# Two DMA transposes of u moved ahead of score transposes on the sync queue, at the start of a fused attention and feed-forward kernel

## The chip, the cores and the metric

One core of one Trainium2 chip. The metric is device time in microseconds (us). Each timing below gives a median and a range over several executions. A kernel and the kernel before it, when compared, ran on the same chip in the same rounds.

"PE" is TensorE's matrix multiply, "PEld" its weight loads, "DVE" is VectorE, "ACT" is ScalarE, "POOL" is GpSimd, and "SP" is SyncE, which here does nothing but issue DMA transposes (and four first loads). Every execution lists the mean granted TensorE clock over its span; 1.000 means that its clock record holds no slowed piece in the span to speak of. (A record can begin late: that of the trace of before begins at 10.4 us and says nothing of the time until then.)

## The reference

Eight batches of attention with squared-ReLU scores, gated by u, then a feed-forward layer with x cos(x):

```python
scores = (1/S) * z @ z.T              # B=8, S=3008, d_qk=64
attn   = maximum(scores, 0) ** 2
x      = u * (attn @ v)               # D=256
h      = x @ w_in                     # 256 -> 2048
out    = (h * cos(h)) @ w_out         # 2048 -> 256
```

The score matrix is symmetric, and the kernel uses that: away from the first batch's first columns it computes only half of the score blocks and gets the rest by DMA transposes.

## The kernel before

The sequence of 3008 rows is cut in six columns of 512 (the last has 448). For each column `c` of batch 0 the scores of blocks (c, R) are computed by PE, passed through ReLU by ACT (or DVE), and squared by DVE into a score buffer `a`. For c = 0, 1, 2 all six blocks are computed directly. Blocks with R = 3, 4, 5 are also transposed, because columns 3 to 5 will use the transposed copy `tt`.

```python
apool = pool("a", 9)        # score buffers
tpool = pool("at", 13)      # transposed score buffers
utpool = pool("ut", 3)      # transposed u
ps_acc = psum("ps_acc", NDH)  # two accumulators, one column at a time
...
def s_squares(b, c, R, p, banks):
    if p == 0:
        halves[(b, c, R)] = apool.tile([P, K, K, P], FP16, name="a")
    t = halves[(b, c, R)]
    ...                                                  # ReLU: rt <- banks
    nc.vector.tensor_tensor(
        t.rearrange("p s k w -> p k s w")[:, 2 * p:2 * p + 2], rv, rv, ALU.mult)
    if p == 1:
        ...
        if R > c and not direct(b, R, c):
            tt = tpool.tile([P, K, K, P], FP16, name="tt")
            turned[(b, c, R)] = tt
            nc.sync.dma_start_transpose(tt..., t...)     # a score transpose
```

A column ends with a multiply by u on DVE, which reads both accumulators out. It needs u with rows and columns exchanged, and that is a DMA transpose on the same sync queue:

```python
def turn_u(b, c):
    ut = utpool.tile([P, NDH, CW], FP16, name="ut")
    hold(nc.sync.dma_start_transpose(ut..., ust[c % 2]...))
    uts[(b, c)] = ut

def finish():      # after the last acc matmul of the column
    ...
    nc.vector.tensor_tensor(x[:, nh, :], acc[nh][:, o:o + n], ut[:, nh, o:o + n], ALU.mult)
```

The program is a list of events, each with a time in abstract units (8 units to a column), emitted in order of that time:

```python
for c in range(NC):
    at(t + c * U + (1 if b or c not in (1, 2) else -3 * c), 0, lambda b=b, c=c: turn_u(b, c))
for q in range(4):
    at(4 + 2 * q, 0, lambda q=q: load_w_in(q))           # loads by POOL
    at(17 + 2.5 * q, 0, lambda q=q: load_w_out(q))
```

In what follows u0, u1, u2 are the transposes of u for columns 0, 1, 2. s1, s2, ... are the score transposes in their order of issue: s1 to s3 are of column 0 (R = 3, 4, 5), s4 to s6 of column 1. With nine score buffers, a square takes the buffer of the square nine places before it. So the square of block (2, 4) needs the buffer that s3 reads from, and the one two places after column 2's last block that of s6. A square cannot start before that transpose has landed.

Of the kernel before, what the change touches and what calls it, by code (L numbers as in the profile page):

```python
# [14 lines left out]
def kernel(  # L15
# [31 lines left out]
    U = 8  # L47
# [37 lines left out]
    def hold(dma):  # L85

        after(dma.ins, gate[0] if gate else before[-1], SYNC)
# [13 lines left out]
    def load_z(b):  # L101
        for g in range(NG):
            n, full, rest = rows(z, b, g)
            j0 = g * G + 1
            load(zst[:, j0:j0 + n, :], full)
            if rest is not None:
                for p0 in (0, JLAST):
                    load(zst[p0:p0 + JLAST, j0 + n, :], rest)

    def turn_z(b):  # L110
        for k in range(2):
            n = (NJ + 2) // 2 - k
            hold(nc.sync.dma_start_transpose(
                zT[b % 2][:, k:k + 2 * n - 1:2, :],
                zst[:, k:k + 2 * n, :].rearrange("p j d -> p (j d)")))

    def load_v(b, g):
        t = vs(b, g)
        n, full, rest = rows(v, b, g)
        load(t[:, 0:n, :], full)  # L120
        if rest is not None:
            for p0 in (0, JLAST):
                load(t[p0:p0 + JLAST, n, :], rest)

    def load_w_in(q):
        fs = slice(q * CW, (q + 1) * CW)
        load(w_in16[:, :, fs], moe_w_in[:, fs].rearrange("(k p) f -> p k f", p=P))

    def load_w_out(q):
        n = NFT // 4  # L130
        load(w_out16[:, q * n:(q + 1) * n, :],
             moe_w_out[q * n * P:(q + 1) * n * P, :].rearrange("(k p) f -> p k f", p=P))
# [3 lines left out]
    def load_u(b, c):  # L136
        r0 = c * CW
        n = min(K, (S - r0) // P)
        st = ust[c % 2]
        for dh in range(NDH):  # L140
            ds = slice(dh * P, (dh + 1) * P)
            load(
                st[:, dh, 0:n, :],
                u[b, r0:r0 + n * P, ds].rearrange("(j p) d -> p j d", p=P))
            if n < K:
                load(st[0:JLAST, dh, n, :], u[b, r0 + n * P:S, ds])

    def turn_u(b, c):
        ut = utpool.tile([P, NDH, CW], FP16, name="ut")
        hold(nc.sync.dma_start_transpose(  # L150
            ut.rearrange("p h (j w) -> p (h j) w", w=P),
            ust[c % 2].rearrange("p h j w -> p (h j w)")))
        uts[(b, c)] = ut
# [17 lines left out]
    def first_z_load(g):  # L171
        zfs[g] = xpool.tile([P, NDH, TW], FP16, name="x")
        zf = zfs[g].rearrange("p h w -> p (h w)").bitcast(FP32).rearrange(
            "p (j d) -> p j d", d=dqk)
        zfs[g] = zf
        n, full, rest = rows(z, 0, g)
        nc.sync.dma_start(zf[:, 0:n // 2, :], full[:, 0:n // 2, :])
        nc.scalar.dma_start(zf[:, n // 2:n, :], full[:, n // 2:n, :])
        if rest is not None:
            nc.scalar.dma_start(zf[0:JLAST, n, :], rest)  # L180
            nc.sync.dma_start(zf[JLAST:P, n, :], rest)

    def first_z_turn(g):
        j0 = g * G
        last = g == NG - 1
        nc.vector.tensor_copy(zst[:, j0 + 1:j0 + 1 + G, :], zfs[g])  # L186
        for k, n in ((0, G), (G, 1))[0:1 + last]:
            tp = ps_w.tile([P, CW], FP32, name="w").bitcast(FP16).rearrange(
                "p (j w) -> p j w", w=P)
            for i in range(n):  # L190
                chain(nc.tensor.transpose(  # L191
                    tp[:, i, :],
                    zst[:, j0 + k + i:j0 + k + i + 2, :].rearrange("p j d -> p (j d)"),
                    ident))
            if g < 2:
                nc.scalar.copy(zT[0][:, j0 + k:j0 + k + n, :], tp[:, 0:n, :])  # L196
            else:
                nc.vector.tensor_copy(zT[0][:, j0 + k:j0 + k + n, :], tp[:, 0:n, :])
# [181 lines left out]
    def at(t, rank, f):  # L380
        events.append((t, rank, len(events), f))
# [11 lines left out]
    for b in range(B):  # L393
        pairs = [(b, c, R, p) for c, R in groups for p in range(2)]
        for i in range(0, len(pairs), NV):
            some = [pr for pr in pairs[i:i + NV] if not direct(*pr[:3])]
            t = b * span - lead + span * i / len(pairs)
# [11 lines left out]
    for b in range(B):  # L409
        for c in range(NC):  # L410
            t = b * span + c * U
# [16 lines left out]
    for m in range(NT):  # L428
        b, i = divmod((m + 1) * TW - 1, S)
# [7 lines left out]
    for b in range(B):  # L437
        t = b * span
        if b == 0:
            for g in range(NG):  # L440
                at(-100 + g, 0, lambda g=g: first_z_load(g))
                at((-30, -2.5, 0.8)[g], 0, lambda g=g: first_z_turn(g))
            first = [lambda: load_v(0, 0), lambda: load_u(0, 0), lambda: load_v(0, 1),
                     lambda: load_v(0, 2), lambda: load_u(0, 1)]
            for i, f in enumerate(first):
                at(-80 + i, 0, f)
            at(-70, 0, gate.clear)
            at(2, 0, lambda: load_u(0, 2))
            for q in range(4):
                at(4 + 2 * q, 0, lambda q=q: load_w_in(q))  # L450
                at(17 + 2.5 * q, 0, lambda q=q: load_w_out(q))
        else:
            at(t - 3.5 * U, 0, lambda b=b: load_z(b))
            at(t - 2.5 * U, 0, lambda b=b: turn_z(b))
            for g in range(NG):
                at(t + (-1.5, -0.4, -0.1)[g] * U, 0, lambda b=b, g=g: load_v(b, g))
        for c in range(3 if b == 0 else 0, NC):
            at(t + (c - 1.25) * U, 0, lambda b=b, c=c: load_u(b, c))
        for c in range(NC):
            at(t + c * U + (1 if b or c not in (1, 2) else -3 * c), 0, lambda b=b, c=c: turn_u(b, c))  # L460
    dummy = kpool.tile([P, 1], FP32, name="dummy")

    def prepare():
# [49 lines left out]
```

## Time and profile before

| kernel before | |
|---|---|
| three runs | 1247.27 us median, 1246.61 to 1248.53 |
| profiled span | 1244.6 us |
| PE busy | 1234.4 us, 99% of the span |
| PE gaps of over 0.15 us between 12 and 75 us | 2.63 us, then 1.33 us in four pieces |
| PE gaps of over 0.15 us after that | none |

The page of the profile of before. The first line is busy time by engine. The other is the chain of work that ended last, as shares of the span (here and below, "issue" is time in which the engine waited for nothing that the profile shows, and DVEq and ACTq are the sequencers of these engines):

```profile
PE 1234.4 (99%) x7533; PEld 680.0 (55%) x7533; DVE 782.0 (63%) x1389; ACT 844.7 (68%) x1609; POOL 145.8 (12%) x201
...
PE 97%; DMA 2%; DVE 0%; ACT 0%; issue 0%; DVEq 0%; ACTq 0%
```

So only PE's few gaps are to be had. The timeline of PE, before. Columns: start, duration, engine, line, operation, out<-in, shapes, count, and in brackets the idle time before it and what ended it:

```profile
38.29 1.46 PE L310 MATMUL acc<-a,v_65 128*128 128x512 f16 x6
39.68 0.60 PE L223 MATMUL w<-zT_63 64*128 64x512 f16 x4
42.91 1.46 PE L310 MATMUL acc<-a,v_66 128*128 128x512 f16 x6 [2.63 <-DVE x L331]
...
61.42 0.45 PE L223 MATMUL w<-zT_63 64*128 64x512 f16 x2 [0.23 <-DVE g L351]
62.62 1.89 PE L344 MATMUL w<-x,w_in_70 128*128 128x512 f16 x8 [0.75 <-DVE g L351]
```

Column 1's last acc matmuls end at 39.75. Column 2 cannot start until the multiply (line 331) has emptied the accumulators. Call this the first gap, and the group at 54 to 63 us the second gap. The timeline of DVE, before, shows why:

```profile
38.42 1.29 DVE L258 TENSOR_TENSOR a<-rt 128x1024 f16<-128x1024 f16 x2 [0.17 <-ACT rt L256]
42.17 1.29 DVE L331 TENSOR_TENSOR x<-acc,ut 128x512 f16<-128x512 f32 x2 [2.46 <-DMA ut<-ust_62]
...
58.88 0.69 DVE L258 TENSOR_TENSOR a<-rt 128x1024 f16<-128x1024 f16 x1 [2.06 <-ACT c_739 L348]
```

The square of block (2, 3) runs at 38.42 without a wait for a transpose. The multiply waits 2.46 us for u1. The last line names ACT's c_739, which this square does not read: line 351 reads it, at 60.69. The ReLU that the square does read had ended by 57.08. c_739 happens to end at 58.80, just as s6 lands, and so the bracket has the wrong name. When a wait is on several semaphores, the chain of waits is the better witness. The chain of waits, before, in order of time (start, duration, what):

```profile
31.03 11.05 DMA ut<-ust_62
...
42.17 0.70 DVE x L331
42.87 0.04 issue
42.91 1.46 PE acc L310 x6
...
47.39 11.40 DMA tt<-a
58.79 0.03 issue
58.82 0.02 DVEq L258
58.84 0.04 issue
58.88 0.17 DVE a L258
```

u1 lands at 42.08 and s6 at 58.79, each just before the work that waited for it.

How DMA transposes and loads get on together shows in the sums by window, before. The columns after the window and its length are PE, PEld, DVE, ACT and POOL busy, granted clock, DMA share (over 1 when packets overlap), and GB/s:

```profile
28.00:38.00 10.00, 10.00 (x53) 3.46 (x52) 8.62 (x14) 7.00 (x14) 0.70 (x1) 1.00 1.35 133
42.00:44.00 2.00, 1.09 (x6) 0.48 (x5) 1.83 (x4) 0.00 (x0) 1.36 (x2) 1.00 1.21 260
```

From 28 to 38 us loads (of w_in, and the last of u2's) and transposes share the engines and move 133 GB/s together. From 42 to 44 us there are only transposes, at 260 GB/s. The Trainium skill, "DMA: Bandwidth & Descriptors", section "Latency and other measured facts", gives 261 GB/s for the DMA transposes of one kernel. These two us agree with it; the trace after moved more, 286 GB/s, from 44 to 46 us, also with transposes alone.

### The profile page before, as it was taken

Reading aid. Unit: us, or ns where it says so; the run is one execution under the profiler, and the core shown is the slowest. Engines: PE = TensorE matmul, PEld = TensorE weight load, DVE = VectorE, ACT = ScalarE, POOL = GpSimd, SP = SyncE. Lnnn points to the kernel's source line nnn. Section 1 sums busy time; section 2 is a strip of 40 time slices with the busy share of each in tenths; the row PEclk is TensorE's granted clock in tenths of the full one; section 3 lists DMA queues with packets and bytes.
Section 4 is the critical chain, followed back from the end, with each engine's and each line's share of the span. In section 5 each row is a group of like instructions: output and inputs, shape, how many; then the busy total and the mean of one; then the engine's idle time right before and its main releaser. Section 6 shows DMA issues by size and latency. Waiting matters only on the chain.

```text
span 1244.6 us, 20404 instructions
## 1 busy us (share of the span) xinstructions
PE 1234.4 (99%) x7533; PEld 680.0 (55%) x7533; DVE 782.0 (63%) x1389; ACT 844.7 (68%) x1609; POOL 145.8 (12%) x201
## 2 busy tenths in 40 slices
PE   9899999999999999999999999999999999999998
PEld 3355555555555555555555555555555555555556
DVE  7766666666666666656666566665666656666555
ACT  6666676666676766667766667766667766667646
POOL 3210101001010010100101011011010111100000
PEclk9999999999999999999999999999999999999999
DMA  9997958679576795757958569685695957957311
GB/s 162 152 174 129 141 91 119 114 122 142 99 117 111 117 144 106 115 111 110 149 101 121 107 109 150 101 129 99 109 158 92 129 101 112 152 101 108 72 33 45
DMA packets 484212, 144.85 MB, mean 116 GB/s; under 512 B 432400, under 2 KB 484112, under 8 KB 484112
## 3 DMA queue, kind: packets, MB, share of 16 engines
q1 hardware_dynamic: 356448, 88.73, 43.1%
q0 software_dynamic: 100400, 29.77, 24.7%
q10 hardware_dynamic: 27264, 25.06, 6.3%
q8 instruction: 59, 0.97, 0.3%
q14 instruction: 41, 0.34, 0.1%
HBM read 60.29 MB, written 24.64 MB: 68 GB/s over the span
## 4 chain that ended last, share of the span: by engine, by line
PE 97%; DMA 2%; DVE 0%; ACT 0%; issue 0%; DVEq 0%; ACTq 0%
PE acc L310 37%; PE w L361 26%; PE w L344 26%; PE w L223 6%; DMA tt<-a 1%; DMA ut<-ust_62 1%; PE acc L285 1%; DMA x<-in_z_dram 0%; DVE g L351 0%; PE w L191 0%; DVE x L331 0%; ACT zT_63 L196 0%; ACT rt L256 0%; DVE a L258 0%; DVE zst L186 0%
## 5 line engine op out<-in xcount | busy, mean ns | idle before, releaser
L361 PE MATMUL w<-w_out_71,g 128*128 128x256 f16 x3008 | 448.6, 273 | 0.0
L344 PE MATMUL w<-x,w_in_70 128*128 128x512 f16 x1504 | 445.6, 379 | 0.8 <-DVE g L351 0.8
L361 PEld LDWEIGHTS <-g 128*128 128x128 f16 x3008 | 294.2, 98 | 191.6 <-issue 1.4
L256 ACT ACTIVATE rt<-w 128x512 f16<-128x512 f32 x489 | 253.1, 613 | 121.2 <-PE w L223 121.2
L258 DVE TENSOR_TENSOR a<-rt 128x1024 f16<-128x1024 f16 x254 | 173.8, 691 | 180.8 <-ACT rt L256 178.3
L344 PEld LDWEIGHTS <-w_in_70 128*128 128x128 f16 x1504 | 147.0, 98 | 59.2 <-issue 3.9
L90 POOL DMA_DIRECT2D ust_62<-in_u_dram x64 | 44.7, 704 | 385.8 <-PE acc L310 355.9
L240 ACT ACTIVATE rt<-w 128x512 f16<-128x512 f32 (+3 forms) x176 | 62.8, 449 | 39.7 <-PE w L223 39.7
L331 DVE TENSOR_TENSOR x<-acc,ut 128x64 f16<-128x64 f32 (+7 forms) x178 | 69.6, 431 | 29.1 <-PE acc L310 26.6
L310 PE MATMUL acc<-a,v_65 128*128 128x512 f16 x336 | 85.8, 380 | 0.0
L310 PEld LDWEIGHTS <-v_66 128*128 128x128 f16 x552 | 51.9, 98 | 61.8 <-issue 14.1
L310 PEld LDWEIGHTS <-v_65 128*128 128x128 f16 x552 | 51.6, 98 | 60.0 <-issue 13.1
L310 PEld LDWEIGHTS <-v_67 128*128 128x128 f16 x552 | 51.9, 98 | 58.7 <-issue 11.1
L310 PEld LDWEIGHTS <-v_68 128*128 128x128 f16 x552 | 51.9, 98 | 57.7 <-issue 10.9
L310 PE MATMUL acc<-a,v_66 128*128 128x512 f16 x312 | 79.4, 379 | 2.6 <-DVE x L331 2.6
L310 PE MATMUL acc<-a,v_68 128*128 128x512 f16 x312 | 79.2, 379 | 0.0
L310 PE MATMUL acc<-a,v_67 128*128 128x512 f16 x312 | 79.1, 379 | 0.0
L368 ACT ACTIVATE ob<-w 128x256 f32<-128x256 f32 x188 | 73.0, 388 | 5.3 <-PE w L361 5.3
L241 DVE TENSOR_TENSOR a<-rt 128x512 f16<-128x512 f16 (+3 forms) x176 | 47.3, 321 | 44.0 <-ACT rt L240 44.0
L90 POOL DMA_DIRECT2D ust_61<-in_u_dram x48 | 36.5, 766 | 224.4 <-PE acc L310 206.7
L310 PE MATMUL acc<-tt,v_68 128*128 128x512 f16 (+1 forms) x240 | 62.2, 371 | 0.0
L310 PE MATMUL acc<-tt,v_67 128*128 128x512 f16 (+1 forms) x240 | 62.1, 371 | 0.0
(1546 smaller groups left out, 1399.8 us busy)
## 6 DMA issues: line engine op xcount, KB each, us to landing
out_dram<-ob ACTq DMA_DIRECT2D x92, 256.0 KB, 2.3
ust_61<-in_u_dram POOLq DMA_DIRECT2D x48, 128.0 KB, 4.0
ust_62<-in_u_dram POOLq DMA_DIRECT2D x32, 128.0 KB, 4.4
a<-a SPq DMA_TRANSPOSE x132, 3.0
v_65<-in_v_dram POOLq DMA_DIRECT2D x4, 512.0 KB, 6.1
v_66<-in_v_dram POOLq DMA_DIRECT2D x4, 512.0 KB, 6.6
v_68<-in_v_dram POOLq DMA_DIRECT2D x4, 512.0 KB, 6.2
v_67<-in_v_dram POOLq DMA_DIRECT2D x4, 512.0 KB, 6.2
```

What stands on the lines that cost most here:

```text
L90: hold(nc.gpsimd.dma_start(dst, src))
L223: chain(nc.tensor.matmul(sp[:, s0 * P:], zt[h, R * K + k + 1 - lo, :], zt[h, j0 + s0:j0 + K, :].rearrange("p j w -> p (j w)"), start=True, ...
L240: nc.scalar.activation(rt[:, i, k * P:], banks[k][:, k * P:], AF.Relu)
L241: nc.vector.tensor_tensor(t[:, k, k:, :].rearrange("p s w -> p (s w)"), rt[:, i, k * P:], rt[:, i, k * P:], ALU.mult)
L256: nc.scalar.activation(rt[:, i, :], banks[k], AF.Relu)
L258: nc.vector.tensor_tensor(t.rearrange("p s k w -> p k s w")[:, 2 * p:2 * p + 2], rv, rv, ALU.mult)
L285: chain(nc.tensor.matmul(accs[(b, c)][nh], vs(b, NG - 1)[h, G - 1, nh * P:(nh + 1) * P], a[h], start=False, stop=False))
L310: chain(nc.tensor.matmul(acc[nh][:, 0:wn], vs(b, j // G)[:, j % G, nh * P:(nh + 1) * P], a, start=(n == 0), stop=(n == NJ - 2)))
L331: nc.vector.tensor_tensor(x[:, nh, :], acc[nh][:, o:o + n], ut[:, nh, o:o + n], ALU.mult)
L344: chain(nc.tensor.matmul(hp, w_in16[:, k, ft * P:(ft + 1) * P], x[:, k, :], start=(k == 0), stop=(k == NDH - 1)))
L361: chain(nc.tensor.matmul(ys[m][:, 0:D], gs[(m, f4)][:, ft % FG, ts * P:(ts + 1) * P], w_out16[:, ft, :], start=(ft == 0), stop=(ft == NFT ...
L368: nc.scalar.activation(obs[m][:, i, :], ys[m][:, 0:D], AF.Copy, bias=0.0, scale=inv_s2)
```

## The change

u1's transpose had its source in place at 18.6 us but was issued at 31.0 us, behind three score transposes. The intent is to issue it, and u2, earlier, so that the multiply never waits.

```diff
-            at(t + c * U + (1 if b or c not in (1, 2) else -3 * c), 0, lambda b=b, c=c: turn_u(b, c))
+            at({(0, 1): 1.01, (0, 2): 6.5}.get((b, c), t + c * U + 1), 0, lambda b=b, c=c: turn_u(b, c))
```

The instruction order on all other engines stays the same. On the sync queue it goes from u0, s1, s2, s3, **u1**, s4, **u2**, s5, s6 to u0, **u1**, s1, s2, s3, **u2**, s4, s5, s6.

## The prediction

> **What bounds the kernel now.** TensorE. The page gives PE 1234.4 of a span of 1244.6 us (99%), at full granted clock; the chain of waits is 97% PE. So nothing can gain more than the few PE gaps. PE's timeline shows, after the start, two: 2.63 us at 40.2-42.9 us (first acc matmul of column 2, released by the gating multiply on DVE), and a cluster at 54-62.6 us (0.20 + 0.16 + 0.23 + 0.75 = 1.34 us, on DVE). After that PE is never idle for over 0.15 us at once.
>
> **First gap.** The multiply of column 1 sat 2.46 us on the transposed u of column 1. That transpose stands behind three score transposes in the sync queue; it is issued at 31.0-35.3 and lands at 42.08. Its source had landed at 18.6. This is what the change aims at.
>
> **Second gap.** In the chain, DVE's square at 58.88 waits for the sixth score transpose (issued 47.4, landed 58.79), which frees a score buffer (of 9). DVE was idle 2.06 us, then ran behind.
>
> **What the change does.** No work is added or removed; only the sync queue's order differs. Before: u0, s1, s2, s3, u1, s4, u2, s5, s6. After: u0, u1, s1, s2, s3, u2, s4, s5, s6. From 17.7 to 80 us this queue issues with hardly a pause (1.2 to 7.4 us each), DMA share mostly above 1: it is bound by throughput. The Trainium skill, "DMA: Bandwidth & Descriptors", section "Issuing engines are not separate DMA queues", says DMAs of all issuers share 16 engines and interleave; the trace agrees: the u2 transpose landed in 3.2 us where no loads ran (42.0), u1's in 11.0 beside the w_in loads.
>
> **Costing.** u1 must wait for its load (18.6), then lands near 22-24, needed at 39.7: -2.6 us. s1-s3 slip by one u transpose (1-4 us). s3 frees the buffer of a square that will be wanted at about 41.3 (43.97 less 2.63); it landed at 41.05, will land near 42: a DVE wait of about 1 us, mostly hidden from PE. Ahead of s6 stands the same set of transposes as before, so it still lands near 58-59.5, while its buffer is now wanted 2.6 us earlier (about 54.2). Also the fourth column's u load, which had waited for u1, and the PE-gated w_out and z loads come earlier and compete. So DVE's wait there grows from 2 to about 4 us, and the PE gaps after it from 1.3 to 2.5-4 us: most of the gain is given back.
>
> **Prediction.** Net -0.9 us: **1246.4 us**, 8 in 10 between **1244.3 and 1248.3** (the runs before spread 1.9 us). Faster by over 2%: 0.01; within 2%: 0.98; slower by over 2%: 0.01.
>
> **What would show it.** Right: u1's transpose lands before 27 us; the multiply no longer waits for it; PE's gap at 40 us is under 1 us; a DVE square waits over 3 us for a score transpose at 54-59 us, and PE's gaps between 44 and 65 us total 2 to 4 us. Wrong: if s6 lands 2 us or more earlier, the second wait does not grow and the full 2.6 us arrives (1244.6). If s3 lands after 43.5, a PE gap stays at 41-44 us.
>
> **What would make it wrong.** How loads and transposes share the DMA engines is judged from one trace; 1-2 us on s6 moves the total one for one. If s6 lands after 60, the kernel is about 1 us slower. A later stage fed by transposes (from 80 us) could start to stall, which I don't expect.

A note on one figure: "where no loads ran" holds from 42 to 44 us; the packets of the next loads began before u2 landed at 45.20.

## The result, and the profile after

1247.86 us median of four runs (1246.64 to 1250.69), against 1247.53 us of four runs of before. A ratio is worked out from the fast runs of the same rounds, so it is not quite the ratio of these medians. It is 1.001, with a 95% interval of 0.9995 to 1.0025: no gain. The forecast gain of 0.9 us did not come. The profiled execution was the fastest of the four.

The timeline of PE, after:

```profile
37.66 1.03 PE L310 MATMUL acc<-a,v 128*128 128x512 f16 x4
38.62 0.60 PE L223 MATMUL w<-zT 64*128 64x512 f16 x4
41.69 2.45 PE L310 MATMUL acc<-a,v 128*128 128x512 f16 x6 [2.46 <-DVE x L331]
44.07 1.04 PE L223 MATMUL w<-zT 64*128 64x512 f16 x4
...
61.71 0.37 PE L223 MATMUL w<-zT 64*128 64x512 f16 x1 [0.25 <-ACT rt L256]
```

The first gap is still there, 2.46 us, released by the same multiply. And the six matmuls after it took 2.45 us, against 1.46 us before. The timeline of DVE, after:

```profile
39.74 1.29 DVE L258 TENSOR_TENSOR a<-rt 128x1024 f16<-128x1024 f16 x2 [2.55 <-ACT rt L256]
40.95 1.28 DVE L331 TENSOR_TENSOR x<-acc,ut 128x512 f16<-128x512 f32 x2
42.15 0.68 DVE L254 TENSOR_SCALAR rt<-w 128x512 f16<-128x512 f32 x1
43.87 1.29 DVE L258 TENSOR_TENSOR a<-rt 128x1024 f16<-128x1024 f16 x2 [1.04 <-DMA tt<-a]
...
57.47 0.69 DVE L258 TENSOR_TENSOR a<-rt 128x1024 f16<-128x1024 f16 x1 [0.28 <-ACT rt L256]
```

The multiply no longer waits for anything of its own. The square ahead of it in DVE's order, block (2, 3), does: 2.55 us. Again the bracket names ACT, whose ReLUs for this block had ended by 37.81, and the chain of waits, after, names the real one:

```profile
23.98 15.67 DMA tt<-a
39.65 0.03 issue
39.67 0.02 DVEq L258
...
40.95 0.69 DVE x L331
41.65 0.04 issue
41.69 2.45 PE acc L310 x6
```

That DMA is s2. It was issued at 23.98 and landed at 39.65; before, the same transpose landed at 27.62. (The last line of DVE above is the square that needs the buffer of s6: it did not wait for it.) The issues of DMA in narrow windows show s2 in both. Columns: out<-in, queue, operation, count, us from issue to landing. Before, a window in which s2 alone is being issued on the sync queue:

```profile
tt<-a SPq DMA_TRANSPOSE x1, 6.5
```

and after:

```profile
tt<-a SPq DMA_TRANSPOSE x1, 15.7
```

The sums by window, after, columns as above, and below it the last of these windows in before:

```profile
28.00:38.00 10.00, 10.00 (x53) 3.51 (x52) 7.80 (x13) 6.86 (x14) 2.19 (x3) 1.00 1.41 118
42.00:46.00 4.00, 4.00 (x14) 1.00 (x12) 2.95 (x6) 1.29 (x3) 0.57 (x1) 0.57 1.38 250
```

```profile
42.00:46.00 4.00, 3.09 (x16) 1.10 (x15) 3.83 (x7) 1.28 (x3) 2.23 (x3) 1.00 0.94 169
```

The granted clock was 0.57 from 42 to 46 us, against 1.00 before. The clock record of the trace has one piece at half speed there, from 42.0 to 45.4 us. The landings of all these transposes, read from the traces (us):

| | u0 | u1 | s1 | s2 | s3 | s4 | u2 | s5 | s6 |
|---|---|---|---|---|---|---|---|---|---|
| before | 21.40 | 42.08 | 23.09 | 27.62 | 41.05 | 43.86 | 45.20 | 52.78 | 58.79 |
| after | 19.61 | 21.88 | 30.73 | 39.65 | 43.77 | 46.17 | 44.44 | 52.34 | 56.99 |

u1 came 20.2 us earlier. s2 came 12.0 us later and s1 7.6 us later. Two things add up for s1. Its issue had to wait behind u1, which had to wait for its own load (landed at 18.80), so it began at 20.53 instead of 17.66 us. And from then on the loads of u2 and w_in were in flight too. For s2 the packets show it. Before, s2 was issued at 21.13 us, and from 20 to 25 us the sync queue moved 0.91 MB and the loads next to nothing. From 25 to 28 us, in both traces, the loads took the DMA engines: a share of 1.30 before and 1.24 after, against 0.14 and 0.05 for the sync queue. After, s2 had only been issued at 23.98 and fell into this stretch.

**Where all the time is decided.** In every trace, the span from the first w_out matmul (line 361) to PE's end is 1168.8 to 1169.3 us. So a kernel's time is settled when that matmul starts, at some 70 us. That start in turn is close to a sum: the start of the first acc matmul, plus PE's gaps, plus half of the time at half clock that falls behind that first matmul (half of it is lost), plus a remainder of 56.1 to 57.3 us in all the traces. Here and in the tables below, gaps are the PE gaps of over 0.15 us summed, and the half clock is that of the first 75 us.

| trace | first acc matmul | gaps 12-50 us | gaps 50-75 us | half clock, us (of it lost: half) | first w_out matmul | span |
|---|---|---|---|---|---|---|
| before | 11.70 | 2.63 | 1.33 | 0 | 72.65 | 1244.6 |
| after | 10.64 | 2.46 | 0.61 | 3.4 | 72.06 | 1244.5 |

After, the profiled execution began 1.06 us earlier; the clock records begin with full speed at 4.4 us in it and at 10.4 us in the trace of before. The repeat of before (below) began at 10.72, so the early start is not the change's. It had 0.72 us less in the second gap, 0.17 us less in the first, and lost 1.7 us to the half clock. Neither the second gap nor the half clock is the change's alone: the repeat of before, too, has a second gap of 0.61 us and 3.4 us of half clock.

### The profile page after: what moved, and what is told of

Same layout as the page of the kernel before. It is cut to its first block, busy times and chain, and to the rows that moved or that the text cites. A ratio compares the mean times of both kernels' runs of the same rounds, so it can differ in the third digit from the quotient of the medians.

```text
span 1244.5 us, 20404 instructions
## 1 busy us (share of the span) xinstructions
PE 1234.8 (99%) x7533; PEld 679.5 (55%) x7533; DVE 782.9 (63%) x1389; ACT 844.9 (68%) x1609; POOL 145.7 (12%) x201
## 4 chain that ended last, share of the span: by engine, by line
PE 97%; DMA 2%; ACT 1%; issue 0%; DVE 0%; DVEq 0%; ACTq 0%
PE acc L310 37%; PE w L361 26%; PE w L344 26%; PE w L223 6%; DMA tt<-a 1%; PE acc L285 1%; ACT rt L256 0%; DMA x<-in_z_dram 0%; ACT zT L196 0%; DVE a L258 0%; PE w L191 0%; DVE zst L186 0%; DVE x L331 0%; ACT c L348 0%; ACT ob L368 0%
## 5 line engine op out<-in xcount | busy, mean ns | idle before, releaser
L348 ACT ACTIVATE c<-w,pihalf 128x512 f16<-128x512 f32 x752 | 496.6, 709 | 224.8 <-PE w L344 213.0
L351 DVE TENSOR_TENSOR g<-w,c 128x512 f16<-128x512 f32 x752 | 495.2, 687 | 191.1 <-ACT c L348 189.6
L361 PE MATMUL w<-w_out,g 128*128 128x256 f16 x3008 | 448.6, 273 | 0.0
L344 PE MATMUL w<-x,w_in 128*128 128x512 f16 x1504 | 445.6, 379 | 0.0
L310 PEld LDWEIGHTS <-v 128*128 128x128 f16 x2208 | 206.6, 98 | 238.8 <-issue 49.7
L310 PE MATMUL acc<-a,v 128*128 128x512 f16 x1272 | 311.7, 381 | 2.5 <-DVE x L331 2.5
L310 PE MATMUL acc<-tt,v 128*128 128x512 f16 (+1 forms) x936 | 226.4, 371 | 0.0
L344 PEld LDWEIGHTS <-w_in 128*128 128x128 f16 x1504 | 146.9, 98 | 59.3 <-issue 2.9
L90 POOL DMA_DIRECT2D ust<-in_u_dram x112 | 81.2, 731 | 600.9 <-PE acc L310 569.7
L223 PE MATMUL w<-zT 64*128 64x512 f16 (+3 forms) x684 | 89.8, 360 | 2.5 <-ACT zT L196 1.1
L240 ACT ACTIVATE rt<-w 128x512 f16<-128x512 f32 (+3 forms) x176 | 62.8, 449 | 39.7 <-PE w L223 39.7
```

What stands on the lines that cost most here:

```text
L90: hold(nc.gpsimd.dma_start(dst, src))
L223: chain(nc.tensor.matmul(sp[:, s0 * P:], zt[h, R * K + k + 1 - lo, :], zt[h, j0 + s0:j0 + K, :].rearrange("p j w -> p (j w)"), start=True, ...
L240: nc.scalar.activation(rt[:, i, k * P:], banks[k][:, k * P:], AF.Relu)
L310: chain(nc.tensor.matmul(acc[nh][:, 0:wn], vs(b, j // G)[:, j % G, nh * P:(nh + 1) * P], a, start=(n == 0), stop=(n == NJ - 2)))
L344: chain(nc.tensor.matmul(hp, w_in16[:, k, ft * P:(ft + 1) * P], x[:, k, :], start=(k == 0), stop=(k == NDH - 1)))
L348: nc.scalar.activation(c16, hp, AF.Sin, bias=pihalf, scale=inv_s2)
```

## The experiments

**Theory A (score buffers).** The first gap changed its owner. u1 in front makes s2 late, s2 holds a score buffer, the square of (2, 3) waits for that buffer, and the multiply stands behind the square on DVE. **Rival B:** the crowding of the DMA engines stalls PE in some way in which score buffers play no part. **Rival C:** the change did gain, and a chance halving of the clock took it.

### First round: the buffers, the loads, and a repeat

`after_again` is the changed kernel unaltered.

> The changed kernel once more, unaltered. Theory A (score buffers): the PE gap near 41 us comes again, 2 to 3 us, released by the multiply of column 1, which stands on DVE behind a square that waits for the second score transpose (landing 38 to 41 us); ratio to before 0.999 to 1.002. Rival C (chance halving of the clock): A gap of 2.5 us is no fixed part of the change; the granted clock at 42 to 46 us is 1.0 this time and the time is about 1.6 us (0.13%) below the profiled run's like for like.

`before_a10` and `after_a10` are the old and the new order with one more score buffer, so that a square waits for the transpose before the one it waited for:

```diff
-    apool = pool("a", 9)
+    apool = pool("a", 10)
```

> The old order with ten score buffers in place of nine. Theory A: the 2.6 us gap at 40 us stays (the multiply waits for u1's transpose, which lands near 42 us), the 1.3 us of gaps at 54 to 63 us go, as the square there takes a buffer freed by an earlier transpose: ratio 0.9985 to 1.0. Rival B (DMA crowding stalls PE in some way that buffers don't touch): both groups of gaps stay, ratio 1.000.

> The new order with ten score buffers. Theory A: the second score transpose lands as late as with nine (38 to 41 us), but no square waits for it; the multiply of column 1 runs at once, the PE gap near 41 us is under 0.3 us, PE gaps from 34 to 66 us total under 0.6 us, the clock stays at 1.0; 3 to 4 us below before, ratio 0.9965 to 0.998. Rival B: the gap stays near 2.5 us and the ratio is 0.999 to 1.001. Rival C: the gap stays, only the halved clock may be missing, ratio 0.999 to 1.0.

`after_wlate` is the new order with the w_in loads emitted later:

```diff
-                at(4 + 2 * q, 0, lambda q=q: load_w_in(q))
+                at(9 + 2 * q, 0, lambda q=q: load_w_in(q))
```

> The new order with nine buffers, and the four loads of w_in emitted five time units later (about 9 us). Theory A with its second half (the score transposes are late because the w_in loads share the DMA engines with them): the second score transpose lands before 33 us instead of at 39.7, so the square does not wait, the PE gap near 41 us goes, ratio 0.9965 to 0.999. If the slip comes from the order alone, it still lands after 37 us and the gap stays at 2 us or more. The loads may come late for their first use near 50 us, then a new PE gap there.

Measured, against before at 1245.25 us median of 11 runs on that chip:

| kernel | median us (range) | ratio (95%) | s2 lands | gaps 12-50 | gaps 50-75 | half clock us | first w_out matmul |
|---|---|---|---|---|---|---|---|
| after_again | 1246.87 (1245.05 to 1250.07) | 1.0015 (1.0002 to 1.0028) | 40.22 | 3.27 | 1.15 | 3.4 | 73.09 |
| before_a10 | 1244.07 (1243.62 to 1246.16) | 0.9995 (0.9982 to 1.0008) | 28.21 | 1.45 | 0.61 | 0 | 69.78 |
| after_a10 | 1245.10 (1242.11 to 1251.55) | 1.0006 (0.9986 to 1.0026) | 41.89 | 1.87 | 2.92 | 10.2 | 77.40 |
| after_wlate | 1247.99 (1242.60 to 1248.80) | 1.0013 (0.9998 to 1.0029) | 32.65 | 0 | 4.62 | 6.8 | 74.63 |

What follows. *after_again*: the gap is a fixed part of the change, again behind the square (3.37 us of DVE waiting for a score transpose) and again with 3.4 us of half clock after it. So rival C falls for the gap. For the half clock a part of it stays, as `before_again` and the closing list show. *before_a10*: as expected by theory A, the first gap stays (1.45 us, on u1) and the second is 0.61 us; the gain in time is within the noise. But 0.61 us is also what `before_again` has with nine buffers, so this trace does not show that the tenth buffer did it. *after_a10*: s2 was as late as ever, but no gap stood at 40 us, as the multiply did not wait:

```profile
38.57 1.28 DVE L331 TENSOR_TENSOR x<-acc,ut 128x512 f16<-128x512 f32 x2
```

That is against rival B. My numbers for this kernel were wrong all the same. Gaps opened at 48 us (1.66 us, behind a square that waited 2.91 us for s3) and at 62 us (1.63 us, behind one that waited 4.13 us for s5, landed at 61.04), each with a half clock. In this trace the gain was given back in other places. It was the slowest execution of the six (1251.55 us; the fastest took 1242.11 us at a clock of 1.000), so it shows what can happen and not what mostly does. The time was unchanged on average.

*after_wlate* shows two things. s2 landed at 32.65 instead of 39.65 us with the same queue order, so its slip is the order together with the w_in loads; and with that the first gap is gone. But then, in this trace (the slowest of its six), the second gap did what the prediction had said of it. The timeline of DVE, w_in late:

```profile
59.29 0.69 DVE L258 TENSOR_TENSOR a<-rt 128x1024 f16<-128x1024 f16 x1 [4.80 <-DMA tt<-a]
```

and that of PE, where eight matmuls that took 1.89 us in before now take 3.46 us on the halved clock:

```profile
60.63 1.85 PE L223 MATMUL w<-zT 64*128 64x512 f16 x4 [3.72 <-DVE g L351]
63.02 3.46 PE L344 MATMUL w<-x,w_in 128*128 128x512 f16 x8 [0.54 <-DVE g L351]
```

s6 landed at 59.19 us, within half a us of the trace of before, though PE had asked for its buffer earlier. As the w_in loads, moved later, now ran beside s4 to s6, this is no clean test of that part of the prediction. The expected gain did not come either: the ratio was 1.0013.

### Second round: one part alone, and another place in the queue

`before_again` is before, unaltered, for a second trace.

> The kernel before once more, for a second trace and for the spread. All theories: one PE gap of 1.5 to 3 us at 40 to 43 us, released by the multiply that waits for u1's transpose (landing 40 to 42.5 us); gaps of 0.6 to 1.4 us at 52 to 63 us; the first w_out matmul starts at 70 to 73 us, and the rest of the span after it is 1168.8 to 1169.4 us. Ratio 0.999 to 1.001.

`u1_only` leaves u2 where it was:

```diff
-            at({(0, 1): 1.01, (0, 2): 6.5}.get((b, c), t + c * U + 1), 0, ...)
+            at({(0, 1): 1.01, (0, 2): 10}.get((b, c), t + c * U + 1), 0, ...)
```

> Only u1 moved ahead (u0, u1, s1, s2, s3, s4, u2); u2 stays where it was. Theory A: all of the new wait comes from u1 standing ahead of s1 to s3, so s2 lands at 38 to 42 us, the square waits for it, the multiply stands behind the square, and the PE gap near 41 us is 2 to 3.5 us, as with the whole change; ratio 1.000 to 1.003. Rival (the move of u2 makes the harm): s2 lands before 34 us, the gap is under 1 us, ratio 0.998 to 0.9995.

`u1_mid` puts u1 between s2 and s3, in the order in which the results are wanted (s2 at 38.4, u1 at 39.7, s3 after that), and leaves u2. `u1_mid_a10` adds the tenth score buffer.

```diff
-            at({(0, 1): 1.01, (0, 2): 6.5}.get((b, c), t + c * U + 1), 0, ...)
+            at({(0, 1): 4, (0, 2): 10}.get((b, c), t + c * U + 1), 0, ...)
```

> u1 between s2 and s3 (u0, s1, s2, u1, s3, s4, u2), nine buffers: each transpose in the order in which its result is wanted. Theory A: s2 lands near 28 us as before, u1 at 34 to 40, s3 at 41 to 44; the PE gap near 41 us falls under 1 us; but the sixth score transpose still lands near 58 us and is wanted near 54, so a PE gap of 2 to 4 us opens at 55 to 63 us, with a halved clock after it in most runs: ratio 0.999 to 1.002. If there is no second wait that takes the gain back, ratio 0.997 to 0.9985.

> The same order with ten score buffers: a square needs the transpose before the one that it needed with nine. Theory A: PE gap near 41 us under 1 us, gaps at 52 to 63 us under 1 us, the clock mostly at 1.0, first w_out matmul at 67.5 to 69.5 us, ratio 0.9965 to 0.9985, the fastest of all so far. If the gain is always given back: a gap of 2 us or more anywhere in 34 to 70 us and ratio 0.999 to 1.001.

Measured, against before at 1246.18 us median of 11 runs:

| kernel | median us (range) | ratio (95%) | s2 lands | gaps 12-50 | gaps 50-75 | half clock us | first w_out matmul |
|---|---|---|---|---|---|---|---|
| before_again | 1246.89 (1245.29 to 1248.10) | 1.0005 (0.9993 to 1.0018) | 27.86 | 3.05 | 0.61 | 3.4 | 72.73 |
| u1_only | 1247.97 (1247.14 to 1250.01) | 1.0016 (1.0003 to 1.0029) | 40.45 | 3.26 | 1.33 | 3.4 | 73.60 |
| u1_mid | 1253.01 (1244.05 to 1257.12) | 1.0037 (1.0005 to 1.0068) | 31.43 | 0 | 0.61 | 6.8 (at the start) | 70.04 |
| u1_mid_a10 | 1243.34 (1242.09 to 1246.34) | 0.9981 (0.9966 to 0.9995) | 32.92 | 0 | 0.61 | 6.8 (at the start) | 70.08 |

*u1_only* repeats the whole change's picture (s2 late, a DVE wait of 3.36 us, the gap 3.26 us), so the move of u1 does the harm, and that of u2 isn't needed for it. *before_again* shows that a half clock can follow the first gap in the kernel before as well. The half clock is therefore a cost of such a gap and not of the new order as such.

Whether a gap of 2 to 3 us pays it hangs in part on chance, by the clock records. In all 14 traces the clock changes stand on a grid of 3.41 us that is placed anew in each execution. After the first acc matmul, each of the nine full-speed windows of this grid in which PE idled for 1.86 to 2.99 us was followed by half clock, and none in which it idled for 1.74 us or less. The 2.63 us of the trace of before fell across two windows, as 0.88 and 1.74 us, and went free; the 2.46 us of after fell into one. That is worked out from the traces, and no run was made to test it.

*u1_mid_a10* was the first kernel clear of before, though the trace of it and that of u1_mid began with half clock from 7.5 to 14.3 us, so that both wanted their data later than usual. That is why its first w_out matmul, at 70.08 us, missed the expected 67.5 to 69.5.

*u1_mid* was odd: two of its six runs took 1244 us and four took 1252 to 1257 us, and the traced one was of the quick kind. Its expectation was missed: the first gap went, but no gap of 2 to 4 us opened at 55 to 63 us in the trace (s6 landed at 53.21), and the ratio was above the stated 0.999 to 1.002.

### Third round: the multiply ahead of the square, and more traces of u1_mid

`after_evict_first` is the changed kernel with the score step of block (2, 3) moved behind the multiply of column 1. Nothing else moves; s2 is as late as before.

```diff
-                    scores.append((c * U + 4 * i / 3 - 3.1, [(b, c, R, 0), (b, c, R, 1)]))
+                    scores.append((15.0 if (c, i) == (2, 1) else c * U + 4 * i / 3 - 3.1,
+                                   [(b, c, R, 0), (b, c, R, 1)]))
```

> The changed kernel, with nine buffers, and the score step whose square waits for s2 moved behind the multiply of column 1 in every engine's order. Theory A: s2 still lands at 38 to 42 us, but the multiply no longer stands behind its square: it starts within 0.3 us of the end of column 1's matmuls (near 38 us), and the PE gap in front of column 2's first acc matmul is under 0.5 us. The late s2 and s3 then show up 2 to 6 us later as another PE gap, as column 2 needs the scores of these squares: gaps from 36 to 50 us still 1.5 to 4 us in total, ratio 0.999 to 1.003. Rival (the multiply or its inputs are slow for another reason): the multiply starts at 40.5 us or later again.

The timeline of DVE, multiply first:

```profile
37.66 1.29 DVE L331 TENSOR_TENSOR x<-acc,ut 128x512 f16<-128x512 f32 x2 [1.15 <-PE acc L310]
38.86 0.68 DVE L254 TENSOR_SCALAR rt<-w 128x512 f16<-128x512 f32 x1
39.84 1.29 DVE L258 TENSOR_TENSOR a<-rt 128x1024 f16<-128x1024 f16 x2 [0.29 <-DMA tt<-a]
44.15 0.69 DVE L258 TENSOR_TENSOR a<-rt 128x1024 f16<-128x1024 f16 x1 [3.02 <-DMA tt<-a]
```

and that of PE:

```profile
39.85 1.47 PE L310 MATMUL acc<-a,v 128*128 128x512 f16 x6
...
45.50 0.39 PE L223 MATMUL w<-zT 64*128 64x512 f16 x2 [1.92 <-DVE rt L254]
45.82 1.68 PE L310 MATMUL acc<-a,v 128*128 128x512 f16 x4
```

The multiply ran at 37.66 us, as soon as its matmuls were done: u1 had long been there, and only the square had stood in its way. Column 2 started, and the late transposes struck 4 us later: a square waited 3.02 us for s3 (landed at 44.06), PE had a gap of 1.92 us, and 3.4 us of half clock followed from 46.1 us. The first w_out matmul started at 72.43 us. The time was 1246.00 us (1245.25 to 1247.43) against 1244.37, ratio 1.0005 (0.9983 to 1.0026). This is what theory A had said: the gap moves, the sum stays.

Two looks at u1_mid:

> u1 between s2 and s3 once more, for another trace, as four of its six timed runs were near 1253 us and the profiled one at 1244. If this run falls in the slow group (over 1250 us): PE gaps between 36 and 66 us of 3 us or more, from waits for score transposes, and 6.8 us or more of halved clock after them, so that the first w_out matmul starts at 78 us or later, and the rest of the span is 1168.8 us as always. If it falls in the fast group: gaps under 1 us and the first w_out matmul near 70 us.

> The same kernel and the same two cases again: a third trace.

They took 1246.49 and 1242.63 us. Neither was of the slow kind, and the first fitted neither branch of what was expected. They differ mainly in s6: it landed at 57.32 in the first (DVE wait 4.02 us, gaps 2.97 us, 3.4 us of half clock, first w_out matmul at 72.35) and at 54.66 in the second (DVE wait 1.53 us, gaps 0.73 us, no half clock, 68.52). In both the first gap was gone. What makes the runs of 1252 to 1257 us was not caught in a trace, and **stays open**. The mean clocks (0.995 to 0.996, against 0.997 in the two quick runs) leave only a small part of it to the clock: time lost to it is (1 - clock) x span, and by that estimate it makes at most 3 of the 8 to 13 us.

### Fourth round: u1 between s2 and s3, ten buffers, again

> u1 between s2 and s3 with ten score buffers, once more, since the first trace of it began with a halved clock (7.5 to 14.3 us) and so wanted its data later than usual. Theory A with a usual start: multiply of column 1 at 38.4 to 39 us without a wait, PE gap there under 0.3 us, gaps from 50 to 66 us under 1 us, first w_out matmul at 67.5 to 69 us; ratio 0.9965 to 0.9985 again. If the first result hung on its slow start: a wait for a score transpose of 2 us or more, a PE gap of over 1 us with a halved clock after it, and a ratio of 0.999 or more.

The timeline of DVE of that kernel:

```profile
37.36 1.29 DVE L258 TENSOR_TENSOR a<-rt 128x1024 f16<-128x1024 f16 x2 [0.17 <-ACT rt L256]
38.58 1.28 DVE L331 TENSOR_TENSOR x<-acc,ut 128x512 f16<-128x512 f32 x2
```

and that of PE, with a gap at neither place of over 0.25 us:

```profile
38.63 0.60 PE L223 MATMUL w<-zT 64*128 64x512 f16 x4
39.31 1.46 PE L310 MATMUL acc<-a,v 128*128 128x512 f16 x6
```

This time the start was usual (first acc matmul at 10.65). s2 landed at 28.23, u1 at 35.89. Gaps were 0 before 50 us and 0.61 us after, the clock stayed at 1.0, the first w_out matmul started at 68.19 us and the span was 1240.1 us, 4.5 us below that of before. The times were 1243.33 us (1241.79 to 1247.51) against 1245.69 us, ratio 0.9993 (0.9977 to 1.0009): two of six runs were near 1247, so this set alone does not show the gain that the first set of the same kernel showed. The traced run was the second fastest of the six. The expected ratio was missed, the expected trace was not.

## Why the prediction was wrong

- **"u1 must wait for its load (18.6), then lands near 22-24"**: right, 21.88 us, and in all later traces of that order 22.1 to 22.9.
- **"needed at 39.7: -2.6 us"**: wrong, and the step that failed. The multiply did stop waiting for u1, but the gap stayed at 2.46 us (3.27 and 3.26 us in further traces), with another transpose as the cause.
- **"s1-s3 slip by one u transpose (1-4 us)"**: the term behind that failure. s3 slipped by 2.7 us and its square waited 1.04 us, as said, but s1 slipped by 7.6 and s2 by 12.0 us. The queue order moved s2 from a time when transposes had the DMA engines nearly to themselves into the time of the loads of u2 and w_in. Moving the w_in loads away brought s2 back to 32.65 us. I had costed a delay on a shared, saturated resource as a constant, where it depended on what else was in flight by then.
- **Looking only at s3's buffer.** I followed the buffer that was late already in the trace of before, and not s2's, which had 10.8 us to spare there (landed 27.62, wanted at 38.42). s2's square stands ahead of the multiply on DVE, so the multiply paid. The runs with ten buffers and with the multiply moved ahead each took that link away, and each removed that gap. s3 then came into play: it had landed after 43.5, which the prediction had named as a sign of a gap at 41 to 44 us, and with s2's link gone its square made gaps of 1.92 us (multiply first) and 1.66 us (ten buffers).
- **"A DVE square waits over 3 us for a score transpose at 54-59 us"**: did not happen in the changed kernel, as its condition (PE arriving 2.6 us earlier) did not arise. s6 landed at 56.99, earlier than I had said. Where the first gap was removed, this wait came in two traces (w_in late, 4.80 us, and one of u1_mid, 4.02 us), and it stayed away in the other two of u1_mid, where s6 landed at 53.21 and 54.66. "It still lands near 58-59.5" had been read from one trace; the repeat of before has s6 at 54.12. So this term is not fixed, and whether a removed first gap is given back differs from one execution to the next.
- **The half clock** was not in the prediction at all: 3.4 us of it after the gap, 1.7 us lost. The Trainium skill, "TensorE: Matmul & The Clock Gate", section "Part 1: The HAM clock gate", says that the clock falls to half after idle windows of about 3.4 us that run freely. The pieces of 3.4 and 6.8 us in these traces agree in length; but PE was idle for only a part of each such window here (see `before_again`, and the list below).
- **The total.** The forecast was -0.9 us with a range that held 1247.86, but the mechanism forecast (first gap gone, second grown) was not the one that happened, so it is luck that the range held the time. By its repeat, 1.0015 (1.0002 to 1.0028), and by u1_only, 1.0016 (1.0003 to 1.0029), the change is if anything a little slower. The traces show no mechanism for that beyond gaps and half clock of about the same size: 3 traces of u1-in-front kernels sum up to 4.8, 6.1 and 6.3 us (gaps plus half of the half clock), two of before to 4.0 and 5.4 us. That is too few to call the difference shown.

## What to carry to other kernels

When a queue that feeds a busy stage is saturated, moving one transfer forward can pass the wait on to those that it overtakes, as it did here, so check the deadline of every transfer that slips, and above all those whose waiters stand ahead of the one you want to help on an in-order engine. Try first the order in which the results are wanted. Here that was u1 between s2 and s3, and it removed the first gap in all five of its traces (none of them of a slow run). In time that is not a shown gain: with nine buffers four of six runs were slower, and with a tenth buffer one set of runs was faster (0.9981) and its repeat was not clear of the noise (0.9993). And when a bracket in a profile names an engine that had long been done, follow the chain of waits to the DMA.

## What the Trainium skill lacked or had wrong

- "TensorE: Matmul & The Clock Gate", section "Why this matters for your kernels", asks for no PE-idle gaps of over about 3 us. Shorter gaps were enough here: half clock followed gaps of 2.46 us (after), 1.92 us (multiply first) and 1.66 us (new order, ten buffers; 1.87 us with a short one in the same window), while one of 2.63 us (before) had none after it. What told them apart in these traces was PE's idle time within one 3.41 us window of the clock record: 1.86 us and more were followed by half clock, 1.74 us and less were not.
- "DMA: Bandwidth & Descriptors", section "Issuing engines are not separate DMA queues", says that transfers of all issuers interleave on the same engines, but not what a transpose loses by it. Here transposes alone moved 260 to 286 GB/s, transposes beside loads 118 to 133 GB/s together (28 to 38 us), and from 25 to 28 us the sync queue's share of the DMA engines was 0.05 to 0.14 against 1.24 to 1.30 for the loads. One score transpose took 6.5 or 15.7 us from issue to landing, depending on what ran beside it and stood ahead of it on its queue.
